# A gated GELU layer on one core: the first 512 rows turned wholly by TensorE and all first loads on one queue, in place of half by transposing DMA and two queues

## The chip, the cores and the metric

The kernel runs on 1 core of one Trainium2 chip. The metric is device microseconds (us) of one execution. The kernel before takes 564.7 us, the median of 3 runs (563.92 to 565.12). Traces are of one profiled execution of the same program.

## The reference

```
x [1, 2048, 1024], w_gate and w_up [1024, 3584], w_down [3584, 1024], all bf16
g = x @ w_gate;  u = x @ w_up
h = gelu_tanh(g) * u
out = h @ w_down
```

## The kernel before

The work is done in two passes (`ip`), each over 1024 rows of x, held as two column blocks `xT[0]` and `xT[1]` of 512 rows. `xT` is x transposed, because TensorE contracts over partitions: 8 blocks (`ko`) of 128 model columns, each 128 x 512. A pass makes `hT` (the hidden values) in 14 units of 256 hidden columns, and then multiplies `hT` by w_down (`down`).

From unit 1 on, a unit is done with seven products of half size in place of eight, with sums of blocks as operands: `t1` to `t4` are sums of blocks of xT (on VectorE), `s1` to `s4` are sums of blocks of the unit's weights. The `s` of unit 1 are made on VectorE, those of every later unit of the first pass on GpSimd (`make_s(ahead, pool)`, L522), a unit ahead. In the first pass GpSimd also makes the sums of w_down for the second half of the work (`keep`, L258): three instructions for each of 14 slices. They go into a tile `m` that has one buffer (L263) or into a spare weight buffer (L261), are stored to DRAM (`store_made`, L269) and are read back in `down` (`load12`, L276; `load4`, L295). Unit 13 makes the last three slices at once.

Unit 0 of the first pass is another case, the "first stage", and it is what the diff touches. It is done plainly, by `plain` (L466) with 64 bf16 matmuls of 128x128 by 128x512: 32 on `xT[0]` into banks 0 to 3, and 32 on `xT[1]` into banks 4 to 7. `finish` (L481) then takes gelu and product. The weights of unit 0 are `wf`, 1 MB, read in three parts along `ko` (`load_wf`, L443); those of unit 1 are `w`, 1 MB (`load_w`, L117).

How the first stage gets its operands before the change:

- SP's queue issues 12 transposing DMAs (`transposing`, L438): blocks 0 to 3 of `xT[0]`, and then all 8 blocks of `xT[1]`.
- ACT's queue issues `wf` blocks 0 to 3, then the right halves (512 columns) of the first 512 rows of x as four tiles `xn` of 128 rows (`load_x`, L422), then `wf` blocks 4 to 7, then `w` of unit 1.
- TensorE turns each `xn` by 4 transposes into one PSUM bank (`turn`, L432), and VectorE (tiles 0 and 2) or ACT (tiles 1 and 3) copies the bank into blocks 4 to 7 of `xT[0]`.

What sets the order. TensorE, VectorE, GpSimd and SP follow the order of the program text. ACT does so inside the `with` block of the first stage (L487); elsewhere a scheduler orders it, except for DMAs that are marked to keep their place (L126, L428, L452). So an ACT copy can't run until the DMAs that stand before it on ACT have been issued. The DMAs of both queues take eight completion counters in turn, and a DMA is issued only when the one eight places before it, on whichever queue, has landed.

Unit 1 then begins with the product `p1` (L188), whose two results ACT copies out (`snap`). After that ACT issues the load of unit 2's weights, w(2) (`aside`, L532 to L535). SP loads w(3) into the buffer of `wf` as soon as the last matmul of unit 0 is done (L524).

Of the kernel before, what the change touches and what calls it, by code (L numbers as in the profile page):

```python
# [10 lines left out]
def kernel(  # L11
# [23 lines left out]
    nc = tc.nc  # L35
    ENG = mybir.EngineType
    ORDER = {ENG.SP, ENG.DVE, ENG.Pool, ENG.PE}
    P = nc.NUM_PARTITIONS
    bf16 = mybir.dt.bfloat16
# [6 lines left out]
    x2 = x.flatten_outer_dims()  # L46
    out2 = out.flatten_outer_dims()
    S, Dm = x2.shape
    Df = w_gate.shape[1]

    NKB = Dm // P
    KH = NKB // 2
# [3 lines left out]
    NS = N // P  # L56
# [19 lines left out]
    def new_x():  # L76
        return [xpool.tile([P, NKB, N], bf16, name=f"xT{c}") for c in range(2)]
# [4 lines left out]
    def slot(shape, dtype, name):  # L82
        return kpool.tile(shape, dtype, name=name, tag="k")


    bank = [psum.tile([P, N], f32, name=f"bank{i}") for i in range(8)]
# [8 lines left out]
    def new(eng, a, b, op, name, shape=None, dtype=None):  # L95
        t = slot(shape or [P, N], dtype or f32r, name)
        eng(t, a, b, op)
        return t

    def cast(src, name, shape=None):  # L100
        t = slot(shape or [P, N], f32r, name)
        nc.scalar.copy(out=t, in_=src)  # L102
        return t
# [6 lines left out]
    def matmul(ps, lhs, rhs, start, stop):  # L110
        nc.tensor.matmul(  # L111
            ps, lhsT=lhs, rhs=rhs, start=start, stop=stop, skip_group_check=True
        )

    def load_w(u, queue=nc.sync):  # L117
        f0 = u * 2 * P
        w = wpool.tile([P, 2, NKB, 2 * P], bf16, name="w")
        for i, src in enumerate((w_gate, w_up)):  # L120
            got = queue.dma_start(
                out=w[:, i],
                in_=src[:, f0 : f0 + 2 * P].rearrange("(ko ki) f -> ki ko f", ki=P),
            )
            if queue is not nc.sync:
                tc.keep_in_program_order(got)  # L126
        return w

# [7 lines left out]
    def sums_t(xT):  # L136
        K = range(KH)
        lo, hi = [[xT[c][:, k] for k in K] for c in range(2)], [
            [xT[c][:, KH + k] for k in K] for c in range(2)
        ]  # L140
        return Sums(
            how={
                "t1": lambda q: [new(dve, lo[1][k], lo[0][k], SUB, "t1") for k in K],
                "t2": lambda q: [new(dve, hi[1][k], q["t1"][k], SUB, "t2") for k in K],
                "t3": lambda q: [new(dve, hi[1][k], lo[1][k], SUB, "t3") for k in K],
                "t4": lambda q: [new(dve, hi[0][k], q["t2"][k], SUB, "t4") for k in K],
                "tb": lambda q: [cast(hi[1][k], "tb") for k in K],
            }
        )

    def sums_s(w, eng):
        GU = range(2)
        sh = [P, KH, P]
        a11, a21 = [[w[:, i, :KH, h : h + P] for i in GU] for h in (0, P)]
        a12, a22 = [[w[:, i, KH:, h : h + P] for i in GU] for h in (0, P)]
        return Sums(
            how={
                "s1": lambda q: [new(eng, a21[i], a22[i], ADD, "s1", sh) for i in GU],
                "s2": lambda q: [new(eng, q["s1"][i], a11[i], SUB, "s2", sh) for i in GU],
                "s3": lambda q: [new(eng, a11[i], a21[i], SUB, "s3", sh) for i in GU],  # L160
                "s4": lambda q: [new(eng, a12[i], q["s2"][i], SUB, "s4", sh) for i in GU],
                "sa": lambda q: [cast(a22[i], "sa", sh) for i in GU],
            }
        )
# [254 lines left out]
    ident = xpool.tile([P, P], bf16, name="ident")  # L419
    make_identity(nc, ident)  # L420

    def load_x(c, queue):  # L422
        t = []
        for i in range(NS):
            xn = slot([P, KH * P], bf16, "xn")
            r0 = c * N + i * P
            got = queue.dma_start(out=xn, in_=x2[r0 : r0 + P, KH * P :])
            tc.keep_in_program_order(got)  # L428
            t.append(xn)
        return t  # L430

    def turn(xT, xn, c, i, copy):  # L432
        tp = bank[4 + i].bitcast(bf16).rearrange("p (k r) -> p k r", k=NKB)
        for ko in range(KH):
            nc.tensor.transpose(tp[:, ko, :], xn[i][:, ko * P : (ko + 1) * P], ident)
        copy(out=xT[c][:, KH:, i * P : (i + 1) * P], in_=tp[:, :KH])  # L436

    def transposing(xT, c, ko, r0):  # L438
        nc.sync.dma_start_transpose(
            out=xT[c][:, ko, :], in_=x2[r0 : r0 + N, ko * P : (ko + 1) * P]  # L440
        )

    def load_wf(queue, k0, k1):  # L443
        for i, src in enumerate((w_gate, w_up)):
            got = queue.dma_start(
                out=wf[:, i, k0:k1],
                in_=src[k0 * P : k1 * P, 0 : 2 * P].rearrange(
                    "(ko ki) f -> ki ko f", ki=P
                ),
            )  # L450
            if queue is not nc.sync:
                tc.keep_in_program_order(got)  # L452

    xT = new_x()
    wf = wpool.tile([P, 2, NKB, 2 * P], bf16, name="w")
    for ko in range(KH):
        transposing(xT, 0, ko, 0)
    load_wf(nc.scalar, 0, 2)
    load_wf(nc.scalar, 2, 4)
    xn0 = load_x(0, nc.scalar)  # L460
    load_wf(nc.scalar, 4, NKB)
    for ko in range(NKB):
        transposing(xT, 1, ko, N)
    w = load_w(1, nc.scalar)

    def plain(ps, c, kos, parts=1):  # L466
        n = N // parts
        for k in range(kos.start, kos.stop, 2):
            for part in range(parts):
                cols = slice(part * n, (part + 1) * n)  # L470
                for p, (j, i) in zip(ps, [(j, i) for j in range(2) for i in range(2)]):
                    for ko in kos[k - kos.start : k - kos.start + 2]:
                        matmul(
                            p[:, cols],
                            wf[:, i, ko, j * P : (j + 1) * P],
                            xT[c][:, ko, cols],
                            ko == 0 and part == 0,
                            ko == NKB - 1,
                        )

    def finish(ps, c):  # L481
        for j in range(2):
            times(j, c, gelu(ps[2 * j]), ps[2 * j + 1])

    on_dve, on_act = nc.vector.tensor_copy, nc.scalar.copy
    s, t = sums_s(w, dve), sums_t(xT)
    with tc.manual_schedule(engines={ENG.Activation}):  # L487
        for _ in range(NWARM):
            nc.tensor.matmul(bank[3], lhsT=warm[:, :P], rhs=warm, start=True, stop=True)
        plain(bank[0:4], 0, range(0, 1))  # L490
        plain(bank[0:4], 0, range(1, 2))
        for i in range(2):
            turn(xT, xn0, 0, i, on_act if i % 2 else on_dve)
        plain(bank[0:4], 0, range(2, 3))
        for i in range(2, NS):
            turn(xT, xn0, 0, i, on_act if i % 2 else on_dve)
        plain(bank[0:4], 0, range(3, 4))
        plain(bank[0:4], 0, range(4, NKB))
        t.make("t1")
        finish(bank[0:4], 0)  # L500
        s.make("s1", "s2")
        t.make("t2", "t3", "tb")
        s.make("s3", "sa")
        plain(bank[4:8], 1, range(NKB))
        finish(bank[4:8], 1)
# [8 lines left out]
    for ip in range(NPASS):  # L514
        for u in range(1 if ip == 0 else 0, NU):
            js = making(u) if ip == 0 else []

            def prepare():
                nonlocal ahead
                nxt["w"], nxt["s"] = ahead, None  # L520
                if u + 1 < NU:
                    nxt["s"] = make_s(ahead, pool)  # L522
                if u + 2 < NU:
                    ahead = load_w(u + 2)  # L524
                if ip == 0:
                    fetch_wd(making(u + 1))
                    for j in making(u - 1):
                        store_made(j)
                for j in js:
                    keep(j, j != js[0])  # L530

            def aside(part):  # L532
                nonlocal ahead
                if ahead is None:
                    ahead = load_w(2, nc.scalar)  # L535
                if part == 0 and "s4" not in s:
                    s.make("s4")
                    t.make("t4")
# [8 lines left out]
            if u + 1 < NU:  # L547
                w, s = nxt["w"], nxt["s"]

        last = ip == NPASS - 1  # L550
        got, nxt = {}, {}
# [22 lines left out]
        if not last:  # L574
            w, t, s = got["w"], got["t"], got["s"]
# [29 lines left out]
```

## Time and profile before

| what | value |
|---|---|
| profiled execution, whole | 564.7 us |
| its span, first to last instruction | 562.9 us |
| median of 3 runs | 564.7 us |
| TensorE (PE) busy | 540.0 us, 96% |
| GpSimd (POOL) busy | 279.5 us, 50% |
| VectorE (DVE) busy | 324.1 us, 58% |
| ACT busy | 243.9 us, 43% |
| mean granted TensorE clock | 0.984 |

All times inside the span are from its start. 1.8 us of the profiled execution lie outside the span. A line of the timeline is: start, duration, engine, source line, operation, tile written<-tile read, shape, count, and in brackets the idle time of that engine just before and what ended it. "SPq" and "ACTq" are the instructions with which SP and ACT issue DMAs. A group of instructions counts as one line where nothing of note lies between them. The windows view lists busy time by engine in each stretch and then the granted clock, the share of the DMA engines and GB/s.

### The profile page before, as it was taken

To read this page: it belongs to the slowest core of one execution; us is meant where nothing else is said; L and a number is where in the kernel's file an instruction comes from. 1 tells how busy PE (TensorE), PEld (TensorE's weight loads), DVE (VectorE), ACT (ScalarE), POOL (GpSimd) and SP (SyncE) were. 2 spreads that over 40 slices of the span, in tenths; PEclk is the share of its full clock that TensorE was granted. 3 is DMA by queue.
4 is the path that set the end of the run, shared out by engine and by line. 5 is a ranking of instruction groups with operands and counts; after the bars stand their busy time and mean duration, and the time that the engine had idled before them with its cause. 6 is when DMAs were issued, how large, how long until landed. Compare 5 with 4: busy or idle time off the path is not lost.

```text
span 562.9 us, 7271 instructions
## 1 busy us (share of the span) xinstructions
PE 540.0 (96%) x2381; PEld 377.2 (67%) x2381; DVE 324.1 (58%) x489; ACT 243.9 (43%) x428; POOL 279.5 (50%) x248
## 2 busy tenths in 40 slices
PE   6799999999999938999999999999999999999997
PEld 2266767777767613688886677777676676478886
DVE  1396555545554696359594555455545557857730
ACT  0545545555555301026536455555455452103441
POOL 0019999999999660000029777667777710000000
PEclk9799999999999978999999999999999999999999
DMA  9585665766755459997936223332222039553751
GB/s 181 118 217 157 169 169 168 195 198 190 194 159 166 134 215 375 296 277 218 306 125 187 76 75 90 112 99 75 76 76 76 0 110 382 200 196 104 212 198 58
DMA packets 110309, 93.28 MB, mean 166 GB/s; under 512 B 19392, under 2 KB 95680, under 8 KB 110272
## 3 DMA queue, kind: packets, MB, share of 16 engines
q1 hardware_dynamic: 103392, 89.15, 54.3%
q10 hardware_dynamic: 6880, 3.67, 2.8%
q8 instruction: 19, 0.31, 0.2%
q14 instruction: 18, 0.15, 0.1%
HBM read 73.92 MB, written 15.20 MB: 158 GB/s over the span
## 4 chain that ended last, share of the span: by engine, by line
PE 60%; DMA 3%; POOL 1%; issue 1%; ACT 0%; SPq 0%; POOLq 0%
PE bank L111 60%; DMA raw<-in_w_down_dram 2%; POOL w L93 1%; DMA td<-w 1%; POOL m L93 1%; DMA td<-m 1%; ACT st L398 0%; SPq L280 0%; POOLq L93 0%
## 5 line engine op out<-in xcount | busy, mean ns | idle before, releaser
L93 POOL TENSOR_TENSOR s<-w 128x512 fp32r<-128x512 bf16 x100 | 116.8, 1187 | 165.5 <-DVE t L90 86.4
L111 PE MATMUL bank<-t,s 128*128 128x512 f32 x648 | 157.0, 398 | 0.0
L111 PEld LDWEIGHTS bank<-t,s 128*128 128x128 f32 x648 | 121.8, 188 | 27.7
L111 PE MATMUL bank<-xT,w 128*128 128x512 bf16 x496 | 121.0, 391 | 6.7 <-ACT xT L436 5.2
L107 ACT COPY p<-bank 128x512 f32<-128x512 f32 x124 | 71.5, 589 | 114.2 <-PE bank L111 114.1
L90 DVE TENSOR_TENSOR hT<-g,bank 128x512 bf16<-128x512 f32 x112 | 76.8, 687 | 65.3 <-ACT g L178 48.8
L111 PEld LDWEIGHTS <-w 128*128 128x128 bf16 x496 | 45.2, 100 | 70.0 <-issue 22.8
L90 DVE TENSOR_TENSOR sum<-bank,p 128x512 f32<-128x512 f32 x54 | 37.3, 692 | 88.0 <-PE bank L111 86.7
L178 ACT ACTIVATE g<-sum 128x512 f32<-128x512 f32 x81 | 51.3, 633 | 55.4 <-DVE sum L90 51.6
L111 PE MATMUL bank<-raw,hT 128*128 128x512 bf16 x224 | 50.9, 388 | 11.2 <-DMA raw<-in_w_down_dram 11.2
L111 PE MATMUL bank<-q 128*128 128x512 f32 x240 | 59.0, 389 | 0.0
L111 PE MATMUL bank<-t,sa 128*128 128x512 f32 x216 | 58.7, 413 | 0.0
L93 POOL TENSOR_TENSOR s<-w,s 128x512 fp32r<-128x512 bf16 x50 | 57.5, 1169 | 0.0
L93 POOL TENSOR_TENSOR s<-s,w 128x512 fp32r<-128x512 f32 x50 | 57.2, 1164 | 0.0
L111 PE MATMUL bank<-tb,s 128*128 128x512 f32 x216 | 53.3, 389 | 0.0
L111 PEld LDWEIGHTS bank<-q 128*128 128x128 f32 x240 | 45.1, 188 | 9.3
L111 PEld LDWEIGHTS <-hT 128*128 128x128 bf16 x224 | 22.1, 100 | 39.4 <-issue 14.8
L111 PEld LDWEIGHTS bank<-t,sa 128*128 128x128 f32 x216 | 40.7, 188 | 10.6
L107 ACT COPY u<-bank 128x512 f32<-128x512 f32 x62 | 35.9, 590 | 24.3 <-PE bank L111 24.2
L111 PEld LDWEIGHTS bank<-tb,s 128*128 128x128 f32 x216 | 40.6, 188 | 8.4
L90 DVE TENSOR_TENSOR q<-hT 128x512 fp32r<-128x512 bf16 x56 | 42.1, 753 | 4.0 <-PE bank L111 4.0
L102 ACT CAST tb<-raw 128x512 fp32r<-128x512 bf16 x28 | 17.3, 626 | 62.1 <-DMA raw<-in_w_down_dram 28.4
(43 smaller groups left out, 454.4 us busy)
## 6 DMA issues: line engine op xcount, KB each, us to landing
raw<-in_w_down_dram SPq DMA_DIRECT2D x80, 256.0 KB, 3.4
q<-td SPq DMA_DIRECT2D x60, 256.0 KB, 5.0
w<-in_w_gate_dram SPq DMA_DIRECT2D x25, 512.0 KB, 4.1
w<-in_w_up_dram SPq DMA_DIRECT2D x25, 512.0 KB, 5.8
td<-m SPq DMA_DIRECT2D x12, 768.0 KB, 4.5
w<-td SPq DMA_DIRECT2D x6, 1024.0 KB, 8.2
out_dram<-st SPq DMA_DIRECT2D x32, 128.0 KB, 1.7
td<-w SPq DMA_DIRECT2D x2, 768.0 KB, 3.8
```

Of the source, the lines that this page charges most:

```text
L90: nc.vector.tensor_tensor(out=out, in0=a, in1=b, op=op)
L93: nc.gpsimd.tensor_tensor(out=out, in0=a, in1=b, op=op)
L102: nc.scalar.copy(out=t, in_=src)
L107: nc.scalar.copy(out=t, in_=ps)
L111: nc.tensor.matmul(ps, lhsT=lhs, rhs=rhs, start=start, stop=stop, skip_group_check=True)
L178: nc.scalar.activation(g, src, ACT.Gelu_apprx_tanh)
```

## The change

All of the first 512 rows of x is loaded untransposed, in four tiles of 128 rows x 1024 columns, from SP's queue, and each is turned by 8 TensorE transposes. Copies 0, 2 and 3 are VectorE's, copy 1 is ACT's, each of twice the size. The three parts of `wf` (now blocks 0-1, 2-4 and 5-7) follow on SP's queue, and then the 8 transposing DMAs of `xT[1]`. The load of unit 1's weights stays on ACT's queue but stands behind ACT's one copy. The first matmuls (blocks 0 and 1) are done in two halves of 256 columns, so that the first half needs only x tiles 0 and 1. Nothing behind the first stage is edited.

```
-    def load_w(u, queue=nc.sync):
+    def load_w(u, queue=nc.sync, pinned=False):
...
-            if queue is not nc.sync:
+            if queue is not nc.sync and not pinned:
                 tc.keep_in_program_order(got)
...
-    def load_x(c, queue):
+    def load_x(c):
         t = []
         for i in range(NS):
-            xn = slot([P, KH * P], bf16, "xn")
+            xn = slot([P, Dm], bf16, "xn")
             r0 = c * N + i * P
-            got = queue.dma_start(out=xn, in_=x2[r0 : r0 + P, KH * P :])
-            tc.keep_in_program_order(got)
+            nc.sync.dma_start(out=xn, in_=x2[r0 : r0 + P, :])
...
-        for ko in range(KH):
+        for ko in range(NKB):
             nc.tensor.transpose(tp[:, ko, :], xn[i][:, ko * P : (ko + 1) * P], ident)
-        copy(out=xT[c][:, KH:, i * P : (i + 1) * P], in_=tp[:, :KH])
+        copy(out=xT[c][:, :, i * P : (i + 1) * P], in_=tp)
...
     xT = new_x()
+    xn0 = load_x(0)
     wf = wpool.tile([P, 2, NKB, 2 * P], bf16, name="w")
-    for ko in range(KH):
-        transposing(xT, 0, ko, 0)
-    load_wf(nc.scalar, 0, 2)
-    load_wf(nc.scalar, 2, 4)
-    xn0 = load_x(0, nc.scalar)
-    load_wf(nc.scalar, 4, NKB)
+    for k0, k1 in ((0, 2), (2, 5), (5, NKB)):
+        load_wf(nc.sync, k0, k1)
     for ko in range(NKB):
         transposing(xT, 1, ko, N)
-    w = load_w(1, nc.scalar)
...
-                    for ko in kos[k - kos.start : k - kos.start + 2]:
+                    for ko in (k, k + 1):
...
-    s, t = sums_s(w, dve), sums_t(xT)
+    t = sums_t(xT)
...
-        plain(bank[0:4], 0, range(0, 1))
-        plain(bank[0:4], 0, range(1, 2))
-        for i in range(2):
-            turn(xT, xn0, 0, i, on_act if i % 2 else on_dve)
-        plain(bank[0:4], 0, range(2, 3))
-        for i in range(2, NS):
-            turn(xT, xn0, 0, i, on_act if i % 2 else on_dve)
-        plain(bank[0:4], 0, range(3, 4))
-        plain(bank[0:4], 0, range(4, NKB))
+        for i in range(NS):
+            turn(xT, xn0, 0, i, on_act if i == 1 else on_dve)
+        w = load_w(1, nc.scalar, pinned=True)
+        s = sums_s(w, dve)
+        plain(bank[0:4], 0, range(0, 2), parts=2)
+        plain(bank[0:4], 0, range(2, NKB))
```

## The prediction

> **What bounds the kernel now.** I read from the end backwards. The chain of waits, in order of time (start, length, what):
>
> ```profile
> 188.23 4.48 issue
> ...
> 196.40 3.19 DMA td<-m
> ...
> 205.79 4.31 DMA td<-w
> ...
> 210.53 11.05 DMA raw<-in_w_down_dram
> ...
> 221.62 338.07 PE bank L111 x1504
> ```
>
> From 221.62 us on TensorE is the chain alone. Before that it stood waiting (9.3 us up to 210.84, then 1.4 and 0.4) for w_down slices that SP could not ask for: in SP's order they stand behind stores of the sums that GpSimd finished at 205.79. So TensorE has some 11 us of slack in the first pass, and GpSimd sets when the second half begins. Next, GpSimd's timeline:
>
> ```profile
> 39.91 1.17 POOL L93 TENSOR_TENSOR s<-w 128x512 fp32r<-128x512 bf16 x1 [38.60 <-DMA w<-in_w_gate_dram]
> ...
> 192.72 1.17 POOL L93 TENSOR_TENSOR m<-raw 128x512 fp32r<-128x512 bf16 x1 [4.49 <-issue]
> ```
>
> Between these it has one gap, 0.64 us at 41.07. The 4.49 us at 188.23 is the one-buffer tile m: its store is issued at 188.26 and such a store (td<-m) lands in 4.5. So the end hangs on the moment when GpSimd starts: when w(2) lands, at 39.91. ACT issues w(2) at 32.65, behind the copies of unit 1's p1, and these follow the first stage's last matmul. Therefore **the first stage's end counts one for one**, although it is 530 us from the end. Now the first stage in the timeline:
>
> ```profile
> 0.74 15.63 SPq L439 DMA_TRANSPOSE xT<-in_x_dram  x12
> 4.96 3.67 PE L111 MATMUL bank<-xT,w 128*128 128x512 bf16 x8 [1.46 <-DMA xT<-in_x_dram]
> ...
> 13.58 0.39 ACTq L445 DMA_DIRECT2D w<-in_w_up_dram  x1
> ...
> 15.26 1.28 ACT L436 ACT_TABLE_LOAD   x1 [15.26 <-issue]
> 16.55 1.07 ACT L436 COPY xT<-bank 128x512 bf16<-128x512 bf16 x2
> ...
> 17.68 16.66 PE L111 MATMUL bank<-xT,w 128*128 128x512 bf16 x64 [5.21 <-ACT xT L436]
> ...
> 32.65 0.37 ACTq L121 DMA_DIRECT2D w<-in_w_gate_dram  x1
> ```
>
> TensorE starts at 4.96, but stands from 12.5 to 17.68 for ACT's two copies. They are late because ACT sat in its own DMA issues until 15.2: the one at 13.58 waited for the eighth DMA before it, a transposing one issued at 8.5 that landed 5.0 us later. The wait costs twice; the windows view (clock in the third column from the right):
>
> ```profile
> 16.00:18.00 2.00, 0.33 (x1) 0.10 (x1) 0.00 (x0) 1.97 (x4) 0.00 (x0) 0.58 1.18 271
> 18.00:20.00 2.00, 2.00 (x6) 0.73 (x5) 0.00 (x0) 0.92 (x1) 0.00 (x0) 0.50 1.41 257
> 20.00:22.00 2.00, 2.00 (x6) 0.69 (x5) 0.00 (x0) 0.00 (x0) 0.00 (x0) 0.50 0.56 139
> 22.00:24.00 2.00, 2.00 (x8) 0.73 (x7) 0.69 (x1) 1.02 (x2) 0.00 (x0) 0.71 0.00 0
> ```
>
> The clock halves at about 16.3 and is whole again at 23.1, so matmuls from 17.68 start 0.428 us apart for 5.4 us, and 0.216 after. The f32 products of unit 1 start at 33.98; 16 bf16 matmuls (p1 and the next product) lie before them, 3.5 us, so **the first stage's matmuls end at about 30.5**.
>
> **The change part by part.**
>
> *Issue on SP.* x, 4 issues at 0.58 (2.32 for 4 on ACT's queue), and wf, 6 at 0.5, from 0.74: done at 6.1. Then 8 transposing issues of 1.26: 6.1 to 16.2. Before, 12 such ended at 16.4. So the transposes of xT[1] leave SP at the same time as before: 4 dear issues go, 10 cheap ones come, and nothing else of SP's stands behind them before 30.9.
>
> *x lands.* A 256 KB load of 2 KB rows (raw) lands in 3.4: first tile 4.1. The next three follow 0.7 apart at the page's best 375 GB/s, or 1.45 at the 181 GB/s of its first slice: last tile 6.2, or 8.5. I take 6.2, since no transposing DMA is ahead of it.
>
> *Turning.* 8 transposes took 0.62 at full clock; 0.9 if halved. The copies double: at most 2 x 0.424 on VectorE, 2 x 0.59 on ACT. Only the last tile's count: x is ready at 6.2 + 0.9 + 0.85 = 8.0 (10.3 at the slow rate). ACT's table load (1.28) now precedes any wait of ACT and lies under the loads. The first half (tiles 0 and 1) can start when wf's first part lands, 6.2 + 0.9 = 7.1, say 7.3.
>
> *wf's rest.* 1 MB at the 300 GB/s of w loads around 36 us: all there at 9.7 (14.3 at 181 GB/s); 16 of the 32 matmuls need the last part.
>
> *Matmuls on xT[0].* From 7.3, at half clock for as long as the rows show: 5.4 us from 17.68; at most 5.2 from 4.96 (matmuls at 10.12 are already 0.26 apart). With 5 us: 11.7 matmuls, then 20.3 at 0.216: end 16.7. Bounds: never halved, 7.3 + 6.9 = 14.2; halved for the whole 6.8 between the clock's two changes and started at 8.2, 18.4. At 181 GB/s, 14.3 + 3.5 = 17.8.
>
> *Matmuls on xT[1].* 32 at 0.216 = 6.9: end 23.6 (21.1 to 25.3). They need the transposes: the last is issued at 14.9 and lands after 3.0 to 7.6 (the rows' range), 17.9 to 22.5; the last 8 matmuls follow, 1.7: 24.2 at worst. About level with the matmuls, so no gain below 21 is likely.
>
> *w of unit 1.* Now behind ACT's copy of tile 1, which ends near 7; before, issued at 14.0 and 14.6, landing after 5.3 and 7.8. Even held until 13.7, when the first transposes have surely landed, it is there at 21.5, before p1 needs it.
>
> *VectorE.* t1 needs blocks 0 to 3 (landed by 14.4 to 17.5); s1 to t3 start when they can after finish, 7 us earlier than at 24.8. t2 needs the last transposes; at 22.5 it would end at 25.0, as s2*t2 comes up at 27.1. What is late here falls on TensorE's 11 us of slack, not on w(2).
>
> *The sum.* 30.5 - 23.6 = 6.9 us. w(3) (at the last plain matmul) and w(2) (behind p1) move by the same amount, with the same crowd of loads around them, so GpSimd starts near 33 in place of 39.91 and the rest follows unchanged. The profiled execution was 564.7, as is the median: **564.7 - 6.9 = 557.8 us**, a span near 556. The bounds 21.1 and 25.3 give 555.3 and 559.5.
>
> *A rule that speaks against it.* The row first: in 8.6 to 12.5, transposes mixed with plain matmuls ran at full clock (8 in 0.62). The Trainium skill ("TensorE: Matmul & The Clock Gate", Part 4: PE-mode transpose) says that transposes don't count as activity for the clock gate. The change puts 32 of them alone ahead of the plain matmuls; by the rule these surely start at half clock, which the sum already has; were the row to hold for transposes alone, an estimate would be 2.5 us better.
>
> **The rivals.**
>
> *Transposes late.* They queue behind 2 MB and beside unit 1's weights; the last two before took 6.9 and 7.6 beside those. If SP's issues are also held by the eighth DMA before each (the last third of wf at 14.3), the last one lands near 25, matmuls end near 27, gain 3.5: 561.2. For it: 7.6 in the row. Against: weights now come early.
>
> *GpSimd does not follow.* TensorE comes earlier, but w(2) lands no sooner because it shares the DMA engines with more: the gain is only more idle at 210, 564.7. For it: w(2) took 7.2 us to land. Against: its companions move with it. A change within 0.2%, about what can be told from nothing here, is this case.
>
> *Slower.* Place: unit 1's weights on ACT's queue. If their issue is held until the last transpose has landed (22.6), they land at about 30.4 (7.8); p1, ACT's casts of w and its copies come after, and w(2) is issued near 34 in place of 32.65: 566.1. It decides from an issue later than about 22. For it: ACT was held 4.6 us once already by such a wait. Against: eight places before them stand wf or early transposes.
>
> **How the numbers follow.** Forecast 0.74 (555.3 to 559.5); late transposes 0.10 (561.2); no follow 0.05 (564.7); slower 0.11 (566.1, or more if ACT's order turns out otherwise further on). Faster 0.84, same 0.05, slower 0.11. The range from 555.0 to 562.0 holds the first two.
>
> **What would show it.** Right: no idle of TensorE over 1 us between 8 and 30; one half-clock stretch ending by 15; f32 products of unit 1 starting near 27; w(2) issued near 25.7 and GpSimd starting near 33; TensorE's wait in the second half still some 9 us, ending near 204. Wrong: xT[0] ready after 12, TensorE waiting for DMA xT past 24, unit 1's weights issued after 20, or GpSimd still starting at 39.

## The result, and the profile after

The changed kernel takes 555.98 us, the median of 4 executions (555.9 to 557.38), beside 564.71 (563.92 to 565.12) for the kernel before: a ratio of 0.9853, with a 95% interval of 0.9834 to 0.9872. The profiled execution went from 564.7 to 557.38, its span from 562.9 to 555.5, 7.4 us less; the numbers below are of that one, the slowest of the four. The forecast was 557.8. Once more, beside other runs, the changed kernel took 556.95 (556.29 to 557.22; `a_again` below).

The first stage of the kernel after, in the timeline (start, duration, engine, line, operation, count, idle before and what ended it):

```profile
0.74 1.81 SPq L427 DMA_DIRECT2D xn<-in_x_dram  x4
...
3.30 1.91 PE L434 MATMUL bank<-ident,xn 128*128 128x128 bf16 x16
...
6.32 10.66 SPq L438 DMA_TRANSPOSE xT<-in_x_dram  x8
6.35 1.89 PE L434 MATMUL bank<-ident,xn 128*128 128x128 bf16 x16 [1.14 <-DMA xn<-in_x_dram]
...
8.03 18.49 PE L111 MATMUL bank<-xT,w 128*128 128x256 bf16 x88
...
10.93 0.46 ACTq L121 DMA_DIRECT2D w<-in_w_gate_dram  x1
...
24.84 0.37 ACTq L121 DMA_DIRECT2D w<-in_w_gate_dram  x1
...
26.17 5.82 PE L111 MATMUL bank<-t,s 128*128 128x512 f32 x24
```

The stall is gone: from 8.03 on the plain matmuls stand in one group, up to the f32 products, which start at 26.17 in place of 33.98 (7.81 earlier). ACT asks for w(2) at 24.84 in place of 32.65, also 7.81 earlier. In the windows view (the clock is the third column from the right) the first of the slow stretches of before is whole, and so are the others:

```profile
16.00:18.00 2.00, 2.00 (x11) 0.94 (x10) 2.00 (x4) 0.36 (x1) 0.00 (x0) 1.00 1.26 193
```

Not every execution of the changed kernel is free of waits here. In that of `a_again` x landed sooner and the plain matmuls began at 6.95, at full rate, but TensorE then stood 1.28 and 0.58 us for transposing DMAs, and the f32 products started at 26.29, no earlier:

```profile
18.84 2.10 PE L111 MATMUL bank<-xT,w 128*128 128x512 bf16 x9 [1.28 <-DMA xT<-in_x_dram]
```

GpSimd's timeline answers to that of before, 7.82 us earlier at its start and 7.85 at unit 13:

```profile
32.09 1.16 POOL L93 TENSOR_TENSOR s<-w 128x512 fp32r<-128x512 bf16 x1 [30.79 <-DMA w<-in_w_gate_dram]
...
184.87 1.16 POOL L93 TENSOR_TENSOR m<-raw 128x512 fp32r<-128x512 bf16 x1 [4.46 <-issue]
```

The chain of waits is the same chain, moved:

```profile
180.41 4.45 issue
...
188.55 3.19 DMA td<-m
...
197.93 4.34 DMA td<-w
...
202.70 11.26 DMA raw<-in_w_down_dram
...
214.00 338.08 PE bank L111 x1504
```

The last restart is at 214.00 in place of 221.62, 7.62 earlier, and 338 us follow it, as before. TensorE's own timeline shows that its wait has kept its size (9.35 us, where before it was 9.3):

```profile
203.08 6.15 PE L111 MATMUL bank<-raw,hT 128*128 128x512 bf16 x16 [9.35 <-DMA raw<-in_w_down_dram]
```

### The profile page after: what moved, and what is told of

It is laid out like the page before. It is cut to its first block, busy times and chain, and to the rows that moved or that the text cites. A ratio compares the mean times of both kernels' runs of the same rounds, so it can differ in the third digit from the quotient of the medians.

```text
span 555.5 us, 7315 instructions
## 1 busy us (share of the span) xinstructions
PE 539.2 (97%) x2405; PEld 380.1 (68%) x2405; DVE 325.1 (59%) x490; ACT 243.5 (44%) x427; POOL 279.4 (50%) x248
## 4 chain that ended last, share of the span: by engine, by line
PE 61%; DMA 3%; POOL 1%; issue 1%; ACT 0%; SPq 0%; POOLq 0%
PE bank L111 61%; DMA raw<-in_w_down_dram 2%; POOL w L93 1%; DMA td<-w 1%; POOL m L93 1%; DMA td<-m 1%; ACT st L398 0%; SPq L280 0%; POOLq L93 0%
## 5 line engine op out<-in xcount | busy, mean ns | idle before, releaser
L111 PE MATMUL bank<-xT,w 128*128 128x512 bf16 (+1 forms) x504 | 117.2, 380 | 0.0
```

What stands on the lines that cost most here:

```text
L111: nc.tensor.matmul(ps, lhsT=lhs, rhs=rhs, start=start, stop=stop, skip_group_check=True)
```

## The experiments

The theory is that of the prediction: the stall came from ACT's copies, held behind DMA issues that waited for a landing. The first experiment adds a second hold, on `wf` itself. And what the first stage gains passes one for one through w(2), GpSimd's start and its chain to the last restart. The rivals: that turning on TensorE is the gain in itself, or that TensorE's work and not GpSimd's chain sets the end. This table is the profiled execution of every run but a_keep4 (its last restart lies 16 matmuls earlier in the work), in us. "Restart" is the last restart of TensorE in the second half.

| kernel | w(2) asked | GpSimd starts | restart | restart - start | time |
|---|---|---|---|---|---|
| before | 32.65 | 39.91 | 221.62 | 181.7 | 564.7 |
| after | 24.84 | 32.09 | 214.00 | 181.9 | 557.38 |
| a_again | 24.96 | 32.16 | 213.86 | 181.7 | 557.22 |
| b_dve | 30.33 | 37.61 | 219.60 | 182.0 | 562.65 |
| b_dve_wfsp | 26.74 | 34.11 | 216.61 | 182.5 | 559.67 |
| a_nowarm | 24.59 | 31.79 | 213.48 | 181.7 | 556.82 |
| a_parts1 | 23.66 | 31.88 | 213.97 | 182.1 | 557.32 |
| a_wfact | 28.06 | 35.73 | 218.05 | 182.3 | 561.4 |
| a_turns | 28.88 | 37.73 | 221.15 | 183.4 | 564.51 |
| a_pool5 | 24.42 | 31.66 | 219.39 | 187.7 | 562.79 |
| a_pe5 | 23.62 | 30.98 | 216.18 | 185.2 | 560.06 |
| a_w2early | 13.61 | 19.83 | 215.87 | 196.0 | 559.22 |
| a_keep | 23.71 | 30.84 | 207.16 | 176.3 | 550.8 |

Time less restart is 343.0 to 343.9 in all of them. In the runs that edit the first stage alone, the restart follows GpSimd's start by 181.7 to 183.4: the one-for-one step, over a spread of 8 us. The last four edit something on the way, and are read one by one. The times given below are medians, with their ranges; the kernel before took 564.1 to 564.5 beside them.

**b_dve: the kernel before, with its two ACT copies given to VectorE.** Nothing else is changed, so ACT's hold can no longer delay xT[0].

```
-            turn(xT, xn0, 0, i, on_act if i % 2 else on_dve)
+            turn(xT, xn0, 0, i, on_dve)
```

The line stands in two places, and both are edited.

> The kernel before, with all four copies of turned x on VectorE in place of two on ACT. Theory: two things were held by ACT's DMA issues, the copies (done 17.6) and the last third of wf (asked at 13.58, landing 3.4 later, 17.0). With the copies gone from ACT, TensorE still stands until about 17.1: clock halves as before, GpSimd starts about 39.3, time 564.1 (0.6 less than 564.7). Rival, the copies alone were the cause: TensorE resumes at 13.4, the clock stays whole, the first stage ends some 6.5 earlier, time 558.

563.19 (562.03 to 565.15); ratio 0.998 (0.9967 to 0.9992). TensorE still stands, for the other thing that the same issue holds, wf:

```profile
13.35 0.39 ACTq L445 DMA_DIRECT2D w<-in_w_up_dram  x1
```

```profile
16.77 3.60 PE L111 MATMUL bank<-xT,w 128*128 128x512 bf16 x10 [2.99 <-DMA w<-in_w_up_dram]
```

The copies had been one of two holds with nearly the same end: 17.68 for the copies before, 16.77 for wf now. GpSimd starts 2.3 us earlier, more than the 0.9 between them: four more matmuls lie ahead of the stand (60 are left after it, up to the f32 products at 31.66, and 64 were left before; 0.9 us), and of what is left 1.9 us is lost to the half clock (14.89 us less 60 x 0.2158) where before it was 2.5 (16.30 less 64 x 0.2158).

**b_dve_wfsp: the same, and the last third of wf asked for by SP,** ahead of its transposing DMAs for xT[1]. Now both holds are lifted, and xT[0] is still half turned by DMA.

```
-    load_wf(nc.scalar, 4, NKB)
+    load_wf(nc.sync, 4, NKB)
```

> As the last, and also the last third of wf (blocks 4 to 7) is issued by SP, between the transposing DMAs of the two column blocks. x is still half turned by DMA and half by TensorE. Theory: neither copies nor wf are held; TensorE resumes near 13.8, the last transposing DMA is issued near 16 and lands by 22, first stage ends near 23.5, GpSimd starts near 33, time about 557.5. Rival, the gain of the change comes from turning x by TensorE itself and not from lifting the hold: time stays near 564.

560.77 (558.41 to 562.47); ratio 0.9935 (0.9913 to 0.9956); 3.3 us above the 557.5 expected. The stand is gone (plain matmuls from 13.24 on without a wait), the f32 products start at 28.08:

```profile
13.24 15.19 PE L111 MATMUL bank<-xT,w 128*128 128x512 bf16 x66
```

GpSimd starts at 34.11. So in the profiled executions lifting the two holds alone brings 5.8 of the 7.8 us (39.91 less 34.11), with no column of x turned by another engine than before. By the medians it brings less, 3.7 us (564.46 less 560.77) of the change's 7.4 to 8.7 (564.32 less 556.95, 564.71 less 555.98), as this profiled execution was 1.1 us faster than its median. The rival that the TensorE turning is the whole gain falls. What is left to it, and to the untransposed loads, is 2 us by the profiles and 4 to 5 by the medians; no run parts these two.

**a_pool5: the changed kernel with GpSimd's two sums s1 of unit 2 made three times** (`again` is 2 for unit 2: four instructions more).

```
+        for _ in range(again):
+            for i in range(2):
+                eng(s["s1"][i], w[:, i, :KH, P:], w[:, i, KH:, P:], ADD)
```

> The kernel after, with the two s1 sums of unit 2 made three times over on GpSimd (four more instructions of 1.12, 4.5 us). Theory, GpSimd's start counts one for one: its work of the first pass ends 4.5 later, TensorE's wait before the second half grows from 9.4 to about 13.9, time 556.0 + 4.5 = 560.5. Rival, TensorE's own work sets the end: 556.0.

561.93 (561.68 to 562.79), 5 to 6 us above the changed kernel for four instructions, 4.5 us, and TensorE waits longer in place of working:

```profile
33.45 5.62 POOL L93 TENSOR_TENSOR s<-w 128x512 fp32r<-128x512 bf16 x5 [0.52 <-DMA w<-in_w_up_dram]
```

```profile
208.44 5.76 PE L111 MATMUL bank<-raw,hT 128*128 128x512 bf16 x16 [11.05 <-DMA raw<-in_w_down_dram]
```

Work added to GpSimd at 33 us is still there at 219. But the wait before the second half grew by only 1.7 us (11.05 for 9.35), where 4.5 was expected: TensorE had already stood 1.54 us at 40.24 for GpSimd's sums and 1.93 at 190.33 for a slice of w_down. The three waits are 14.5 us together, 5.2 more than the 9.35. Of the 0.5 to 1.4 us beyond the four instructions, 1.1 is seen in GpSimd's last nine (14.10 us for 13.03), as those into m now run beside VectorE's sums at 1.6 us each.

**a_pe5: unit 1's second product done four times on TensorE,** behind w(2)'s request (24 matmuls more, 5.2 us).

```
-            product(c[i], w[:, i, KH:, :P], b21, True)
+            for _ in range(4 if snap_first else 1):
+                product(c[i], w[:, i, KH:, :P], b21, True)
```

> The kernel after, with the second product of unit 1 made four times over on TensorE (24 more bf16 matmuls, 5.2 us), behind the request for w(2). Theory, TensorE has slack in the first pass: its wait before the second half shrinks from 9.4 to about 4.2, time 556.0, within 1 us. Rival, TensorE's own work sets the end: 561.2.

560.35 (558.75 to 563.08): between the two expectations, 3.4 to 4.4 us above the changed kernel. TensorE's slack is there (the 9.35 us wait shrank to 6.18), but it is not free. GpSimd started at 30.98, 1.1 earlier than after, and had lost 2.1 us of that by its seventh instruction (9.57 us after its start, where after it is 7.43), in five instructions beside VectorE's sums, of which these are two:

```profile
34.28 3.19 POOL L93 TENSOR_TENSOR s<-s,w 128x512 fp32r<-128x512 f32 x2
```

```profile
33.21 6.36 DVE L90 TENSOR_TENSOR t<-xT,t 128x512 fp32r<-128x512 bf16 x4
```

In the kernel after, VectorE made the same four sums at 29.53 in 2.49 us, before GpSimd had begun, and GpSimd's pairs took 2.30. TensorE's delay had pushed VectorE's sums under GpSimd's, and both slowed. GpSimd lost 1.59 more at 179.79, waiting for a store of m. SP issues such stores in order with loads of w_down, and two of these were held for VectorE's sums, 7.1 us together, which follow TensorE's products.

**a_w2early: w(2) asked for in the middle of the first stage.** This would start GpSimd long before TensorE's copies of p1.

```
         finish(bank[0:4], 0)
+        ahead = load_w(2, nc.scalar, pinned=True)
...
-    ahead = None
```

> The kernel after, with w(2) asked by ACT right behind the two gelus of the first stage (near 16.4) in place of behind p1 (24.84); its buffer is free from the start. Theory, GpSimd's start sets the end: w(2) lands near 22 to 24, GpSimd starts 8 to 10 earlier than 32.09, loses some 2 to 4 of it where VectorE is busy beside it, and TensorE's wait before the second half shrinks from 9.4 to 2 to 4; time 549 to 551. Rival, GpSimd can't run ahead of TensorE (its tiles are freed by TensorE): 556.

559.28 (557.88 to 561.54): above the changed kernel, where the theory expected some 6 us below. In this form the theory fell. GpSimd does start at 19.83, 12 us earlier, and then:

```profile
24.61 3.16 POOL L93 TENSOR_TENSOR s<-s,w 128x512 fp32r<-128x512 f32 x2
...
38.59 1.45 POOL L93 TENSOR_TENSOR s<-w 128x512 fp32r<-128x512 bf16 x1 [4.55 <-PE bank L111]
```

It works beside VectorE at 1.6 us an instruction, and at 38.59 it waits for TensorE. TensorE had itself waited 2.52 us at 22.96 for a transposing DMA, beside which w(2) now landed:

```profile
22.96 0.58 PE L111 MATMUL bank<-xT,w 128*128 128x512 bf16 x1 [2.52 <-DMA xT<-in_x_dram]
```

GpSimd's way to the restart is 14.1 us longer than in the kernel after (196.0 for 181.9). The 4.55 are part of it, and 5.1 are four waits for stores of m, the longest 3.40 at 179.47; the rest lies in the slower instructions and in the second half of w(2), which GpSimd awaits 2.14 us in place of 0.66.

So "GpSimd's start sets the end" holds only while GpSimd is behind: what it makes is consumed by TensorE in turn, and it can't run ahead. The first stage's end moves both; w(2) alone doesn't.

**a_nowarm: without the five warm-up matmuls** (`NWARM = 0`).

> The kernel after without the five warm-up matmuls. Theory, the TensorE transposes alone release the clock: they still run at half rate and the plain matmuls from about 8 are 0.216 apart from the first or nearly so; first stage ends within 0.7 of 22.7, time 556.0. Rival, transposes don't count and the five matmuls did it: plain matmuls run at half rate for 3.4 to 6.8 from 8.0, first stage ends 1.7 to 3.4 later, time 557.7 to 559.4.

556.78 (555.88 to 557.87), not to be told from the changed kernel; the f32 products start at 25.92, and full rate comes near 10.0, where in the kernel after it comes near 10.2. Here the transposes do what the warm-ups were there for.

**a_parts1: without the halving of the first matmuls** (no `parts=2`).

> The kernel after with the first 16 half matmuls as 8 whole ones. Theory: they must wait for the fourth copy, 8.96 in place of 8.03, so all of TensorE is 0.9 later, GpSimd starts 0.9 later, time 556.9. Rival, the halves cost as much in their 8 more weight loads as they save: 556.0.

556.68 (556.26 to 557.32), not told apart from the changed kernel either. In its profiled execution x happened to land earlier (32 transposes without a gap, over at 7.0) and the matmuls then waited 0.92 for VectorE's copy; they ran at full rate from the first. So what the halving is worth stays open, below about 1 us.

**a_wfact: wf asked for on ACT's queue,** beside x on SP's: first loads on two queues again.

```
-        load_wf(nc.sync, k0, k1)
+        load_wf(nc.scalar, k0, k1)
```

> The kernel after with wf issued from ACT's queue, x and the transposing DMAs from SP's: two queues again, x still turned whole by TensorE. Theory, the number of queues is not the cause: the transposing DMAs are issued 3 earlier, which hides behind the matmuls, x and wf share the DMA engines so that x is turned some 1 later; first stage ends near 23.5, time 556 to 557. Rival, loads split over two queues are what held the kernel before: ACT's copy and w(1) are held until the first transposes have landed, first stage ends 3 or more later, 559 or more.

560.72 (559.48 to 561.68). The rival's number came, by a hold in another place. ACT's copy wasn't held (it ran at 6.17), but SP's fourth issue of x was, for the first DMA of wf, which ACT had issued at 0.73 and which landed 3.3 us later. In the waits view (engine, line, awaited, us in total, times, longest):

```profile
SPq L427 <- DMA w<-in_w_gate_dram: 2.0, 1, 2.0
```

So SP's four issues of x took 3.64 us in place of 1.81, and the last tile, beside wf, landed 5.8 us after its issue in place of 4.9:

```profile
9.86 1.04 PE L434 MATMUL bank<-ident,xn 128*128 128x128 bf16 x8 [1.92 <-DMA xn<-in_x_dram]
10.69 19.05 PE L111 MATMUL bank<-xT,w 128*128 128x256 bf16 x86
```

The last tile is turned at 9.86, where it was at 7.3 in the kernel after, and the plain matmuls run at half their rate until about 14. Of the 2.6 us by which the last tile is later, some 1.9 is the held issue and the rest the slower landing. So of the change's parts, that all first loads stand in the order of their use on one queue is worth about 4 us (560.72 beside 556.78 and 556.68 for the two kernels above, of the same set of runs). The Trainium skill ("DMA: Bandwidth & Descriptors", Issuing engines are not separate DMA queues) says that spreading loads over SP and ACT brings no bandwidth, only issue time; here it cost time, as the last part of the load wanted first was held for a landing of the load wanted later, and then shared the engines with it.

**a_turns: no warm-ups, and each transpose done four times,** 128 in a row, to see what transposes alone do to TensorE's rate (one execution).

> The kernel after without warm-up matmuls and with each of the 32 TensorE transposes made four times over: 128 transposes in a row from 3.4 on and no matmul before them. Theory, transposes release the clock: within 6.8 us, before 10.2, their spacing falls from 0.107 to about 0.06, and they end before 14. Rival, they don't count: 0.107 throughout, end at 17.1, and the plain matmuls behind them start at 0.43.

```profile
3.26 9.94 PE L434 MATMUL bank<-ident,xn 128*128 128x128 bf16 x128 [3.26 <-DMA xn<-in_x_dram]
```

In the windows view of the transposes alone (TensorE's busy time, and in brackets how many ran in each microsecond):

```profile
7.50:8.50 1.00, 1.00 (x12) 1.00 (x11) 1.00 1.21 293
8.50:9.50 1.00, 1.00 (x18) 1.00 (x17) 1.00 1.96 182
9.50:10.50 1.00, 1.00 (x22) 1.00 (x20) 1.00 0.88 178
```

Their rate doubles near 8.8, 5.5 us after the first of them, and no other matmul has run by then. At the pace of the kernel after (16 in 1.91) 128 would take over 13 us; they took 9.94. The 88 plain matmuls after them run at full rate from the first (17.52 us in place of 18.49). The time, 564.51, is 7 us up: the f32 products start 4.0 later than after, and w(2) lands 8.9 us after it was asked for in place of 7.3, so that TensorE waits for it; what else adds to the 7 us stays open.

A fixed time after the start doesn't explain it: full rate came near 6.6 in a_again and a_parts1, whose 32 transposes ran almost without a gap, near 10.2 in the kernel after and near 14 in a_wfact, whose transposes come in four groups. What exactly TensorE must do for it, and for how long, is not shown.

**a_again: the changed kernel, unaltered,** of the same set of runs as a_turns and the two that follow.

> The kernel after once more, unchanged, beside the next two on one chip: 556.0, within 1.

556.95 (556.29 to 557.22), ratio 0.9867 (0.9852 to 0.9883).

**a_keep: an edit that the chain points to.** In unit 13 GpSimd waits 4.46 us at 184.87 because the first of its three last slices goes into the one tile m, whose store is out. It is made last here, and the two that go into spare buffers first; the stores follow in the same order.

```
-                for j in js:
+                for j in js[1:] + js[:1]:
                     keep(j, j != js[0])
...
-                for j in making(NU - 1):
+                last_js = making(NU - 1)
+                for j in last_js[1:] + last_js[:1]:
                     store_made(j)
```

> The kernel after with the three last slices of w_down's sums made and stored in another order: the two in spare buffers first, the one in the tile m last, so that GpSimd does 8 us of work while m's store lands in place of waiting 4.5 for it. Nothing of the first stage is touched. Theory, the chain through GpSimd's work of the first pass sets the end: GpSimd ends some 4.5 earlier (193.5 in place of 197.9), TensorE's wait before the second half shrinks from 9.4 to about 5, time 551.5. Rival, TensorE waits there for the transfers themselves: 556.

550.79 (550.48 to 551.39); ratio to the kernel before 0.9762 (0.9743 to 0.978). The wait is gone from GpSimd, and TensorE's wait falls from 9.35 to 3.79:

```profile
179.26 7.29 POOL L93 TENSOR_TENSOR w<-w 128x512 fp32r<-128x512 bf16 x6
186.51 1.60 POOL L93 TENSOR_TENSOR m<-raw 128x512 fp32r<-128x512 bf16 x1
```

```profile
196.40 6.20 PE L111 MATMUL bank<-raw,hT 128*128 128x512 bf16 x16 [3.79 <-DMA raw<-in_w_down_dram]
...
207.16 10.52 PE L111 MATMUL bank<-raw,hT 128*128 128x512 bf16 x48 [0.46 <-DMA raw<-in_w_down_dram]
```

The restart is 6.7 us earlier than in a_again (207.16 for 213.86), the median 6.2. Of the 6.7, 4.5 is the wait, 1.1 that the last nine instructions took 11.99 us in place of 13.05, as fewer of them run beside VectorE's sums, and 1.3 that GpSimd happened to start earlier (30.84 for 32.16), which is not the edit's. This is the fastest version found: it confirms the chain of waits as the bound by taking a link out of it.

**a_keep4: a_keep, and the three stores issued at step 4 of the second half,** so that w_down's slices ahead of it aren't behind them. The lines below stand in place of the same three under step 0.

```
+            if step == 4:
+                last_js = making(NU - 1)
+                for j in last_js[1:] + last_js[:1]:
+                    store_made(j)
```

> As a_keep, and SP issues the three stores four steps later, behind two more loads of w_down slices. Theory: TensorE goes on for two more slices (8 matmuls each, 3.4 us in all) before it stands, and its wait shrinks to some 2: time 549. Rival: the sums read back later hold up what follows by as much: 551.5, as a_keep.

552.5 (551.87 to 553.43), 1.7 more than a_keep, though GpSimd also started 1.15 later in its profiled execution (31.99). TensorE now does 48 matmuls before it stands, in place of 32, but then stands longer, 7.21 in place of 3.79:

```profile
203.75 16.20 PE L111 MATMUL bank<-raw,hT 128*128 128x512 bf16 x64 [7.21 <-DMA raw<-in_w_down_dram]
```

The stores land later, the read-back of the sums on SP's queue waits for them, and the w_down slices behind the read-back come later by as much: the rival's reading.

## Why the prediction was right, and where it was off

*The bound* was right. GpSimd's chain ended the first pass before and after, with nearly the same waits (4.49 and 4.46 for m, 9.29 and 9.35 on TensorE), and a_pool5 and a_keep moved the time by adding to it and taking from it.

*One for one* was right for the first stage: 7.81 us off its end became 7.82 at GpSimd's start, 7.62 at the restart, 7.4 in the span.

*The cause of the stall* was right, with one thing missing: the text named ACT's copies as what ended the idle time, as the profile did. b_dve shows that wf's last third, held at the same place on ACT, would have ended it little earlier: in the kernel before it was asked for at 13.58 and landed 3.4 us later, some 0.7 before the copies were done. The profile names only the releaser that came last.

*Issue on SP:* x took 0.45 an issue, not 0.58, and the transposing issues ran from 6.32 to 16.98, for 6.1 to 16.2.

*x lands* was off: the tiles were taken 0.7 us apart. Tiles 1 and 2 landed 2.5 and 2.8 us after their issue, 3 and 4 only 4.7 and 4.9. TensorE turned the last two from 6.35 on, and the first plain matmul came at 8.03 in place of 7.3: 0.7 us lost. Of wf, all was there at 10.3, for 9.7, and TensorE didn't wait for it; 12 of the 32 matmuls read its last part, not 16.

*The half-clock term* was the mis-sized one. The text took 5 us at half rate, 2.5 us lost. The plain matmuls took 18.14 us from 8.03 to 26.17 for 80 of full size (88, of which 16 are halves); at 0.2158 each that is 17.26, so 0.88 us was lost, less than 2 us at half rate. The 5.4 us that it was sized by lay after a long stand, and the 5.2 after a start in which TensorE had done only warm-ups. What the sum left out is that the 32 transposes work towards the full clock too, which a_turns shows and a_nowarm agrees with. The text had weighed the rule of the Trainium skill ("TensorE: Matmul & The Clock Gate", Part 4: PE-mode transpose) that transposes don't count for the clock gate; a_turns contradicts it for these transposes, and the measurement decides: 1.6 us of the error is here. The row that was set against the rule had been read too widely: its four transposes at 8.65 still ran at half rate (0.61 us for 4), and full rate begins only near 9.9. The term also varies: in a_again and a_parts1 full rate came before the first plain matmul, and nothing was lost.

*The end of the first stage's matmuls:* 26.17 less 16 matmuls, 3.5, is 22.7 in place of 23.6. The 0.7 lost at the start and the 1.6 won at the clock give that 0.9.

*Last transposes* (rival 1): the last two landed near 20.4 and 20.9, 6.0 and 5.2 us after their issue, in the range of 17.9 to 22.5, and in this execution TensorE didn't wait for them. The text's "about level with the matmuls" was the better reading, though: in a_again, the same kernel, TensorE stood 1.28 and 0.58 us for transposes (under 1 us had been named as a sign of being right), and in a_w2early, with one more load beside them, 2.52 at once. In a_again the earlier start of the matmuls won nothing.

*GpSimd does not follow* (rival 2) fell: GpSimd started 7.25 us after w(2) was asked for, and 7.26 before.

*w of unit 1* (rival 3): the first of its issues was held to 10.93. Eight places ahead of it stands the first transposing DMA, issued at 6.32, which landed near 10.9: the hold that the rival feared, but from an early transpose, and harmless at 10.93 as its limit was about 22.

*"What is late here falls on TensorE's 11 us of slack"* was wrong as a general claim, though nothing of it was called on here. a_pe5 put 5.2 us on that slack and lost 3 to 4 us, since a late TensorE pushes VectorE's sums under GpSimd's.

*The number* is in part luck. 557.8 lies 0.4 above the profiled execution and 1.8 above the median, and two errors of opposite sign, 0.7 at the start and 1.6 at the clock, went into it. The terms above are those of the profiled execution; what made the other three 1.4 us faster is in no trace.

## What to carry to other kernels

When an engine stands for a copy, look at what the copying engine's queue did before: a DMA issue that waits for an older landing holds everything behind it, computing work too, and the landing can be that of another queue's DMA. Take away all that one hold delays, since the profile names only the one that ended last; and order first loads by use on one queue. Slack of an engine is not free when its delay moves another engine's work under that of the critical one.

## What the runs showed of the hardware that was not expected

- **Transposes alone bring TensorE to full rate:** 128 of them from 3.26 on doubled their rate near 8.8 us. The granted clock reads 1.00 in these first microseconds all the same; the low rate at the start shows only in the counts per microsecond (12, then 22).
- **VectorE and GpSimd slow each other when both read two operands from SBUF:** a 128x512 sum went from about 0.62 to 1.59 us on VectorE (2.49 and 6.36 for four) and from 1.15 to 1.6 on GpSimd (2.30 and 3.19 for two). In a_pool5 GpSimd kept 1.14 an instruction beside VectorE's sums with an operand in PSUM, which stayed at 0.69. The Trainium skill ("SBUF — State Buffer", SBUF: two separate sides) tells of a lock on a port that the two share, for VectorE operations with two SBUF inputs; the runs agree with it in kind, and give the price.
- **Of four 256 KB loads issued 0.45 us apart, the last two landed some 2 us later** after issue than the first two (2.5, 2.8, 4.7, 4.9). It differs from run to run by about 1 us (3.7 and 4.0 for the last two in a_again); what sets it stays open.
